# The first token group of an mLSTM and SwiGLU kernel: k and q of both halves loaded first, the weight loads all asked for by SP, and the first group's steps in another order

## The chip, the cores and the metric

The kernel runs on one core of one Trainium2 chip. The metric is the device time in microseconds (us) of one execution. The kernel before takes 515.06 us, the median of three runs (513.95, 515.06, 515.78).

## What is computed

An mLSTM cell over 4 batches, 8 heads, 768 tokens and 40 features, and a SwiGLU block on its output:

```python
for t in range(S):
    m_new = np.maximum(f_gate[:, :, t] + m, i_gate[:, :, t])
    f_stab = np.exp(f_gate[:, :, t] + m - m_new)
    i_stab = np.exp(i_gate[:, :, t] - m_new)
    C = f_stab * C + i_stab * outer(vt, kt)
    n = f_stab * n + i_stab * kt
    y[:, :, t] = sigmoid(o_gate[:, :, t]) * (C @ qt) / max(|n . qt|, 1)
...
x = y as (3072 tokens, 320)
out = (silu(x @ w_gate) * (x @ w_val)) @ w_out      # 320 -> 1536 -> 320
```

q, k, v and the gates arrive as float32, the three weight matrices as float64, that is as pairs of 32-bit words.

## The kernel before, in words

**Groups.** The 768 tokens of a batch are cut into six groups of 128. All four batches of a group are worked on together, so that a group has 32 heads (batch times head) and 512 tokens for the SwiGLU block. The 32 heads stand in two halves of 16, called P = 0 and P = 1 (the "pairs" of the change: two batches each); batch u has 8 of them. Group 0 starts from an empty state and has its own functions (first_...); groups 2 to 5 run in a steady loop at the end, which the change doesn't touch.

**Order.** The order of the instructions on every engine is the order of the program text (manual_schedule): each engine and each DMA-asking engine (SP, and in places ACT) takes its own instructions in that order and waits at each for what it needs. A DMA that SP can't ask for yet holds up all those that SP asks for later.

**Group 0.** f0 and i0 hold the gates of the first 128 tokens. From their sums and running maxima PE builds the exponents of the weight table in PSUM (first_mask, first_inputs, first_maxima), and ACT writes the exponentials into W0, which lies in the first eight rows of h_sb (first_exp). k and q of 16 heads are turned by PE (first_turn with 128x128 transposes; turn_one, used by group 1, with 64x64 ones) and copied to kT and qT. first_scores multiplies k and q on PE, and DVE multiplies the scores into W0. first_own multiplies W0 with the values v of batch u, first_x divides (DVE), first_gate multiplies by the sigmoid of o (sig, ACT), first_wrap's copy repeats 64 columns behind x, and a seam turns x on PE and copies it to xT. first_values and first_state make the state that group 1 starts from. burn(n) issues n products of zeros in bf16 that nobody reads.

**PSUM.** There are eight banks in two rings of four, tagged "cell" and "gen"; a bank is taken again when the work on its previous content is done.

**Weights.** The weights come in ten pieces, piece_load(p): pieces 0 and 1 hold one block (128 columns of w_gate and w_val, 640 KB in three DMAs), pieces 2 to 6 two blocks (1,280 KB in three DMAs), pieces 7 to 9 parts of w_out (1,280 KB in one DMA). w_gate goes into partitions 0 to 63, w_val into 64 to 127. A piece lands either in one of two rotating "raw" buffers or in a tile that is not in use yet (home). Block j is then rebuilt as float32 by convert(j): scale (ACT, two operations), join (DVE, two) and rounded (one integer addition on GpSimd or DVE).

**The blocks of group 0's SwiGLU.** hidden(0, m) multiplies xT with block m (L706, 20 records on PE), ACT takes the Silu (L711) and DVE the product (L712) into h_sb. Twelve such steps m = 0 to 11 run one after the other; in each, the conversions that ahead[m] names come before the Silu, and what slots[m] names comes behind: the preparation of group 1. Of that matter here: late_sums, late_maxima and late_decay (sums and maxima of the gates of tokens 128 to 767, from f_sb and i_sb), M_dram (the maxima written to DRAM by SP, L963), weights_load (SP reads M_dram back, spread over 64 partitions, into the two partition halves of w_sb, L484), turn (k and q of group 1, slots 5 and 6), weights_sub and weights_mask in slot 7 (DVE L488, GpSimd L493), weights_exp in slot 8 (ACT L512), the scores and weigh in slot 9 (PE L353, DVE L360), and do_add in slot 10 (PE L379). Then follow the remaining blocks, the projection (project_all, L723) and the loop over the later groups.

**Functions and lines that are spoken of:** load (L138), piece_load (L187), scale, join, rounded (L212 to L229), late_sums (L296 to L298), turn_one (L318), first_values (L552, L553), first_turn (L561), first_scores (L571, L575), first_own (L582), first_x (L587 to L590), first_gate (L596, L597), first_state (L604), first_seam (L616), sig (L515), burn (L521).

Of the kernel before, what the change touches and what calls it, by code (L numbers as in the profile page):

```python
# [18 lines left out]
L = 128  # L19
# [5 lines left out]
def kernel(  # L25
# [111 lines left out]
    def load(dst, a, c, P):  # L137
        nc.sync.dma_start(out=dst[:, heads(P), 0:D], in_=tokens(a, c, P))  # L138
# [7 lines left out]
    def gate_rows(a):  # L146
        return a.rearrange("b h s -> (b h) s")
# [3 lines left out]

    nc.scalar.dma_start(out=f0, in_=spread_rows(f_gate))
    nc.sync.dma_start(out=i0, in_=spread_rows(i_gate))
    nc.scalar.dma_start(out=flat(f_sb), in_=gate_rows(f_gate)[:, L:])
    nc.scalar.dma_start(out=flat(i_sb), in_=gate_rows(i_gate)[:, L:])


    raws = {}
    PIECES = [("gv", 0, 1), ("gv", 1, 1)] + [("gv", m, 2) for m in range(2, NFC, 2)] + [("o", m, 4) for m in range(0, NFC, 4)]

    def piece_load(p, home=None):
        kind, m, n = PIECES[p]
        if kind == "gv":
            a, d = NKC, n * 128
            gate_w, val_w = (w[:, m * 128:(m + n) * 128].rearrange("(c p) f -> p c f", p=HP) for w in (moe_w_gate, moe_w_val))
            src = [(slice(0, HP), slice(0, NKC), gate_w), (slice(HP, 128), slice(0, NKC - 1), val_w[:, 1:]),
                   (slice(HP, 128), slice(NKC - 1, NKC), val_w[:, 0:1])]
            queues = (nc.sync,) + 2 * (nc.scalar if p < 5 else nc.sync,)
        else:
            a, d = n, DM  # L170
            src = [(slice(0, 128), slice(0, n), moe_w_out[m * 128:(m + n) * 128].rearrange("(a p) d -> p a d", p=128))]
            queues = (nc.sync,)
        if src[0][2].dtype == F32:
            for r, cs, w in src:
                if kind == "o":
                    nc.sync.dma_start(out=wo_sb[r, m:m + n, :], in_=w)
                else:
                    for x in range(n):
                        nc.sync.dma_start(out=wgv_sb[r, m + x, cs], in_=w[:, :, ts(x, 128)])
            return  # L180
        if home is None:
            raw = conv.tile([128, 4 * NKC * 128], U32, name="raw")
        else:
            raw = home.rearrange("p a t -> p (a t)").bitcast(U32)
        raw = raw[:, 0:2 * a * d]
        for (r, cs, w), queue in zip(src, queues):
            queue.dma_start(out=raw[r].rearrange("p (a d) -> p a d", a=a)[:, cs], in_=w.bitcast(U32))  # L187
# [43 lines left out]
    def convert(j, eng=None):  # L231
        scale(j)
        join(j)
        rounded(j, eng)

    for P in range(2):
        load(k_sb, k, 0, P)
        load(q_sb, q, 0, P)
        load(v_sb, v, 0, P)
    load(o_sb, o_gate, 0, 0)  # L240


    junk = early.tile([128, 512], BF16)
# [51 lines left out]
    def late_sums():  # L295
        nc.vector.tensor_tensor_scan(flat(f_sb), flat(keep1), flat(f_sb), 0.0, op0=ALU.mult, op1=ALU.add)  # L296
        nc.gpsimd.memset(step1, 0.0)
        nc.gpsimd.tensor_sub(i_sb, i_sb, f_sb)  # L298

    def late_maxima():  # L300
        nc.vector.tensor_copy(step1[:, 0:1, 0:1], f0[0:BH, end].unsqueeze(1))
# [8 lines left out]
    M_dram = tc.dram_tile([BH, S - L], F32, name="M_dram")  # L310


    def turn_one(P, src, dst, engs):
        tp = [bank("tp_kq").rearrange("p (a t) -> p a t", t=SUB) for _ in range(2)]
        for a in range(UA):
            h = P * UH + 2 * a
            for i in range(2):
                nc.tensor.transpose(tp[i][:, a, :], src[half(i), h:h + 2, :].rearrange("p h d -> p (h d)"),  # L318
                                    ident[half(i), half(i)])
        for i in range(2):  # L320
            copy(engs[i], dst[:, P * UA:(P + 1) * UA, half(i)], tp[i])
# [143 lines left out]
    def xT(n):  # L465
        return xT_sb

    def seam(n, P, engs):
        engs = list(engs)
        dst = xT(n).rearrange("p c (u i s) -> p c u i s", u=B, i=2)  # L470
        for cs in (range(0, 4), range(4, NKC)):
# [76 lines left out]

    w_end = early.tile([128, BH, 1], F32)

    def first_values(P):
        nc.gpsimd.tensor_copy(w_end[:, heads(P)], W0[:, heads(P), end])  # L552
# [26 lines left out]
    def first_own(u):  # L579
        first_y[u] = bank("first_y", "gen")[:, 0:H * D1].rearrange("p (h d) -> p h d", d=D1)  # L580
        for h in range(H):
            nc.tensor.matmul(first_y[u][:, h, :], lhsT=W0[:, u * H + h, :], rhs=v_sb[:, u * H + h, :], start=True, stop=True)  # L582

    def first_x(u):
        y = first_y.pop(u)
# [21 lines left out]
    def first_kept(P, ps, eng):  # L607
        copy(eng, state(2)[:, P * UA:(P + 1) * UA], ps)

    def first_seam(P, engs):  # L610
        for c, eng in zip(range(0, NKC, 2), engs):
            cs = range(c, min(c + 2, NKC))
            tp = bank("tp_x")[:, 0:len(cs) * 2 * L].rearrange("p (c u s) -> p c u s", u=2, s=L)
            for w in cs:
                for b in range(2):
                    nc.tensor.transpose(tp[:, w - c, b, :], x_sb[:, 2 * P + b, ds(w * HP, 2 * HP)], ident)  # L616
            copy(eng, xT(0)[:, c:c + len(cs), 2 * P * L:(2 * P + 2) * L].rearrange("p c (u s) -> p c u s", u=2), tp)
# [12 lines left out]
    first_own(0)  # L630
    late_sums()
    first_turn(1, k_sb, kT, (A, A))
    first_x(0)
    first_turn(1, q_sb, qT, (A, V))
    load(o_sb, o_gate, 0, 1)
    piece_load(0)
    first_own(1)
    first_values(1)
    first_scores(1)
    first_x(1)  # L640
    sig(0)
    piece_load(1)
    burn(3)
    first_own(2)
    piece_load(2, h_sb[:, 1:1 + NKC])
    sig(1)
    burn(2)
    first_own(3)
    first_gate(0)
    first_x(2)  # L650
    first_x(3)
    first_gate(1)
    first_seam(0, (A, A, V))
    scale(0)
    ps1 = first_state(1, "gen")
    burn(1, "gen")
    piece_load(3, h_sb[:, NH - NKC:])
    join(0)
    first_seam(1, (A, A, V))
    rounded(0, V)  # L660
    first_kept(0, first_state(0), A)
    first_kept(1, ps1, V)
    convert(1, V)
    nc.scalar.activation(warm, warm, AF.Silu)
    piece_load(4, wo_sb)
    piece_load(5)


    pair = early.tile([BH, PP], F32)
# [289 lines left out]
    def load_all(dst, a, n):  # L959
        for P in range(2):  # L960
# [147 lines left out]
```

## Time and profile before

| what | value |
|---|---|
| median of three runs | 515.06 us (513.95 to 515.78) |
| the profiled execution's own time | 513.3 us |
| its span, first to last instruction | 511.5 us |
| PE (matmul) busy | 505.1 us, 99% |
| PE weight loads busy | 428.8 us, 84% |
| DVE / ACT / GpSimd busy | 332.3 / 204.8 / 255.0 us |
| DMA moved | 43.27 MB in 205,497 packets, 193,432 of them under 512 B |
| first product of group 0's SwiGLU (L706) | 31.92 us |

The profile is one execution on the chip; times are from the span's start. PE is TensorE's matmuls, PEld its weight loads, DVE VectorE, ACT ScalarE, POOL GpSimd, SP the engine that asks for DMAs; a trailing q is an engine's sequencer. A row of a timeline has start, busy time, engine, line, operation, what is written and read, the count, and in brackets the idle time ahead of it with what ended it. A row of the windows view has the stretch, its length, the busy time of each engine with the number of instructions, PE's granted clock, the DMA engines' mean busy share (packets overlap, so it can be over 1) and GB/s. q, k, v and o come in rows of 160 bytes, the weights in rows of 1,024 or 2,048, so a transfer of the same size can take different times. "To landing" in the view of DMA issues is the time from an issue to the last part of its data.

### The profile page before, as it was taken

The page shows a single profiled execution, that of the slowest core. Times are in us where ns is not written, and L with a number is a line of the kernel's source. Part 1 is how long each engine was busy: PE and PEld are TensorE (multiplying, and loading weights), DVE is VectorE, ACT ScalarE, POOL GpSimd, SP SyncE. Part 2 cuts the span into 40 slices and gives each one's busy share as a digit, 9 for nine tenths or more (in the row PEclk, how much of TensorE's full clock was granted, in tenths as well). Part 3 has the DMA queues.
Part 4 walks back from the last instruction along what each step waited for, and adds up shares of the span by engine and source line. Part 5 has one row for each costly group of instructions (what it writes and reads, how often), then busy time and mean ns, then how long its engine had stood idle before and what let it go on. Part 6 is the DMA issues. An engine that isn't in the chain of part 4 may idle for free.

```text
span 511.5 us, 14788 instructions
## 1 busy us (share of the span) xinstructions
PE 505.1 (99%) x6307; PEld 428.8 (84%) x6309; DVE 332.3 (65%) x539; ACT 204.8 (40%) x394; POOL 255.0 (50%) x274
## 2 busy tenths in 40 slices
PE   8999999999999999999999999999999999999997
PEld 4964445667888899988899888899988899988896
DVE  5779767887897777687466678467658554233421
ACT  3477655448512339312339321338421340223210
POOL 1303427475879663367652457652447650166710
PEclk9999999999999999999999999999999999999999
DMA  9999999698502992501993411993101200000001
GB/s 123 174 232 238 168 194 244 148 177 119 88 1 45 143 130 39 92 3 26 156 134 42 75 21 27 156 131 43 42 3 19 37 3 27 27 1 0 1 14 38
DMA packets 205497, 43.27 MB, mean 85 GB/s; under 512 B 193432, under 2 KB 200600, under 8 KB 205432
## 3 DMA queue, kind: packets, MB, share of 16 engines
q1 hardware_dynamic: 203444, 39.49, 49.4%
q10 hardware_dynamic: 1988, 2.85, 2.4%
q8 instruction: 49, 0.80, 0.7%
q14 instruction: 16, 0.13, 0.1%
HBM read 35.68 MB, written 4.01 MB: 78 GB/s over the span
## 4 chain that ended last, share of the span: by engine, by line
PE 91%; DMA 2%; DVE 2%; issue 1%; POOL 1%; ACT 1%; SPq 0%; DVEq 0%; ACTq 0%; POOLq 0%
PE gv_x L854 26%; PE o_ps L777 23%; PE gv_y L854 21%; PE gv_ps L706 5%; PE o_ps L723 5%; DMA w_sb<-M_dram 2%; PE inter L402 2%; PE intra L411 2%; PE sp L353 2%; PE first_y L582 1%; PE add L379 1%; POOL w_sb L493 1%; PE burn L521 1%; PE tp_kq L561 1%; PE sp L571 1%
## 5 line engine op out<-in xcount | busy, mean ns | idle before, releaser
L854 PE MATMUL gv_x<-xT,wgv_sb 64*128 64x256 f32 x720 | 89.1, 377 | 0.0
L854 PEld LDWEIGHTS gv_x<-xT,wgv_sb 64*128 64x128 f32 x720 | 69.6, 187 | 7.9 <-issue 0.2
L777 PE MATMUL o_ps<-wo_sb,h_sb 128*128 128x160 f32 x480 | 67.4, 300 | 0.0
L777 PEld LDWEIGHTS o_ps<-wo_sb,h_sb 128*128 128x128 f32 x480 | 65.6, 190 | 1.7 <-issue 1.7
L902 ACT ACTIVATE h_sb<-gv_x 128x256 f32<-128x256 f32 x30 | 11.5, 383 | 117.8 <-PE gv_x L854 117.8
L706 PE MATMUL gv_ps<-xT,wgv_sb 64*128 64x512 f32 x240 | 53.7, 596 | 0.3 <-DVE wgv_sb L229 0.3
L706 PEld LDWEIGHTS gv_ps<-xT,wgv_sb 64*128 64x128 f32 x240 | 23.6, 187 | 24.4 <-issue 23.2
L854 PE MATMUL gv_y<-q_sb,wgv_sb 64*128 64x256 f32 x360 | 44.0, 377 | 0.0
L854 PE MATMUL gv_y<-xT,wgv_sb 64*128 64x256 f32 x360 | 43.9, 376 | 0.0
L854 PEld LDWEIGHTS gv_y<-q_sb,wgv_sb 64*128 64x128 f32 x360 | 34.9, 187 | 4.2 <-DVE tmp L894 0.4
L854 PEld LDWEIGHTS gv_y<-xT,wgv_sb 64*128 64x128 f32 x360 | 35.0, 187 | 3.9
L364 POOL TENSOR_TENSOR vw_sb<-v_sb,w_sb 128x656 f32<-128x656 f32 x10 | 14.6, 1467 | 41.2 <-ACT w_sb L509 40.0
L777 PE MATMUL o_ps<-wT,S 128*128 128x160 f32 x240 | 33.4, 299 | 0.0
L777 PEld LDWEIGHTS o_ps<-wT,S 128*128 128x128 f32 x240 | 32.9, 190 | 0.0
L509 ACT ACTIVATE w_sb<-w_sb,g_T 128x64 f32<-128x64 f32 x128 | 31.0, 334 | 0.0
L854 PE MATMUL gv_x<-q_sb,sw 64*128 64x256 f32 x240 | 31.0, 376 | 0.0
L875 POOL TENSOR_TENSOR h_sb<-x_sb 128x512 f32<-128x512 f32 x12 | 15.8, 1314 | 24.6 <-ACT x_sb L874 24.6
L895 POOL TENSOR_TENSOR tmp<-tmp 128x512 f32<-128x512 f32 x15 | 20.0, 1332 | 14.5 <-DVE tmp L894 14.5
L875 POOL TENSOR_TENSOR h_sb<-tmp 128x512 f32<-128x512 f32 x13 | 16.5, 1269 | 21.5 <-ACT tmp L874 21.5
L744 POOL TENSOR_TENSOR S<-h_sb 128x256 f32<-128x256 f32 x30 | 22.6, 752 | 9.2 <-DVE h_sb L875 7.3
L854 PE MATMUL gv_y<-q_sb,sw 64*128 64x256 f32 x200 | 27.0, 388 | 0.0
L723 PE MATMUL o_ps<-wo_sb,h_sb 128*128 128x320 f32 x96 | 26.9, 437 | 0.0
(221 smaller groups left out, 984.6 us busy)
## 6 DMA issues: line engine op xcount, KB each, us to landing
w_sb<-M_dram SPq DMA_DIRECT2D x10, 512.0 KB, 7.1
k_sb<-in_k_dram SPq DMA_DIRECT2D x12, 320.0 KB, 7.4
v_sb<-in_v_dram SPq DMA_DIRECT2D x12, 320.0 KB, 5.5
o_sb<-in_o_gate_dram SPq DMA_DIRECT2D x12, 320.0 KB, 6.8
raw<-in_moe_w_out_dram SPq DMA_DIRECT2D x3, 1280.0 KB, 7.5
x_sq<-k_sb SPq DMA_DIRECT2D x64, 40.0 KB, 2.0
q_sb<-in_q_dram SPq DMA_DIRECT2D x32, 64.0 KB, 3.8
out_dram<-tmp SPq DMA_DIRECT2D x24, 80.0 KB, 1.7
```

Source lines behind the costliest of these rows:

```text
L353: nc.tensor.matmul(sp[two][half(i), a, :], lhsT=kT[feats(two), P * UA + a, half(i)], rhs=qT[feats(two), P * UA + a, half(i)], start=True, ...
L364: eng.tensor_tensor(vw_sb[:, heads(P)], v_sb[:, heads(P)], w_sb[:, heads(P), last].to_broadcast([128, UH, D1]), op=ALU.mult)
L402: nc.tensor.matmul(inter[two][half(i), a, :], lhsT=qT[feats(two), P * UA + a, half(i)], rhs=state(2 * n + i)[feats(two), P * UA + a, :], s ...
L509: nc.scalar.activation(w_sb[:, h], w_sb[:, h], AF.Exp, bias=g_T[:, n, h:h + 1], scale=-1.0)
L706: nc.tensor.matmul(ps[i], lhsT=wgv_sb[half(i), m, kc, :], rhs=x[half(i), kc, :], start=(kc == 0), stop=(kc == NKC - 1))
L723: nc.tensor.matmul(ps[u], lhsT=hid(g, m)[:, ts(u, L)], rhs=wo_sb[:, m, :], start=(m == 0), stop=(m == NFC - 1))
L744: eng.tensor_tensor(S1[:, k], lo[:, second_half], hi[:, second_half], op=ALU.add)
L777: nc.tensor.matmul(node[x][:, i], lhsT=lhs(k)[:, ts(i, L)], rhs=rhs(k), start=start and k == 0 and i == 0, stop=stop and k == KH - 1, skip ...
L854: nc.tensor.matmul(ps[:, i, cols], lhsT=lhs(c)[half(i)], rhs=rhs(c)[half(i)], start=start and c == 0, stop=stop and c == n - 1, skip_group ...
L875: (nc.vector if k == KH - 1 else nc.gpsimd).tensor_tensor(h_sb[:, 2 * k + 1], uw[:, 0], uw[:, 1], op=ALU.mult)
L895: nc.gpsimd.tensor_tensor(uw[:, :, second_half], uw[:, :, second_half], uw[:, :, first_half], op=ALU.add)
L902: nc.scalar.activation(h[:, first_half], x[:, 0, first_half], AF.Silu)
```

## The change

Loads: the gates of the later tokens (f_sb, i_sb) go from the front of ACT's queue to a place behind piece 1 on SP; k and q of both halves are asked for first, then v of both, then o's first half, piece 0, o's second half, piece 1, the later gates, and pieces 2, 3 and 4. All of these are asked for ahead of any work, and all parts of every piece by SP (before, ACT asked for w_val of pieces 0 to 4, each piece at a place between the steps of group 0). Piece 1 shares piece 0's raw buffer; piece 2's home is the back part of wo_sb. Piece 5 moves to slot 0.

Steps: the scores of both halves come ahead of the products with the values; the second half is turned by turn_one; first_own does each head in two column halves; half of the gates go to GpSimd; the seam is made of 64x64 transposes; late_sums, late_maxima, M_dram, late_decay, late_turns and decay move to later slots.

```diff
-    nc.scalar.dma_start(out=flat(f_sb), in_=gate_rows(f_gate)[:, L:])
-    nc.scalar.dma_start(out=flat(i_sb), in_=gate_rows(i_gate)[:, L:])
...
-            queues = (nc.sync,) + 2 * (nc.scalar if p < 5 else nc.sync,)
+            queues = (nc.sync,) + 2 * (nc.sync,)
...
-            raw = conv.tile([128, 4 * NKC * 128], U32, name="raw")
+            if p == 1:
+                raw = ring[0][:, 2 * NKC * 128:]
+            else:
+                raw = ring[p] = conv.tile([128, 4 * NKC * 128], U32, name="raw")
...
+    for dst, a in ((k_sb, k), (q_sb, q)):
+        load(dst, a, 0, 0)
+    for dst, a in ((k_sb, k), (q_sb, q)):
+        load(dst, a, 0, 1)
     for P in range(2):
-        load(k_sb, k, 0, P)
-        load(q_sb, q, 0, P)
         load(v_sb, v, 0, P)
     load(o_sb, o_gate, 0, 0)
+    spare_wo = wo_sb.rearrange("p m d -> p (m d)")[:, H * L:H * L + 4 * NKC * 128].rearrange("p (a t) -> p a t", a=1)
+    for p, home in ((0, None), (1, None), (2, spare_wo), (3, h_sb[:, NH - NKC:]), (4, None)):
+        piece_load(p, home)
+        if p == 0:
+            load(o_sb, o_gate, 0, 1)
+        if p == 1:
+            nc.sync.dma_start(out=flat(f_sb), in_=gate_rows(f_gate)[:, L:])
+            nc.sync.dma_start(out=flat(i_sb), in_=gate_rows(i_gate)[:, L:])
...
-        nc.gpsimd.tensor_sub(i_sb, i_sb, f_sb)
+        nc.vector.tensor_sub(i_sb, i_sb, f_sb)
...
-            nc.tensor.matmul(first_y[u][:, h, :], lhsT=W0[:, u * H + h, :], rhs=v_sb[:, u * H + h, :], start=True, stop=True)
+            for i in range(2):
+                nc.tensor.matmul(first_y[u][half(i), h, :], lhsT=W0[:, u * H + h, half(i)], rhs=v_sb[:, u * H + h, :],
+                                 start=True, stop=True)
...
-    def first_gate(P):
-        for u in (2 * P, 2 * P + 1):
-            x = x_sb[:, u, 0:DM].rearrange("p (h d) -> p h d", d=D)
-            nc.vector.tensor_tensor(x, x, o_sb[:, u * H:(u + 1) * H], op=ALU.mult)
+    def first_gate(u, eng):
+        x = x_sb[:, u, 0:DM].rearrange("p (h d) -> p h d", d=D)
+        eng.tensor_tensor(x, x, o_sb[:, u * H:(u + 1) * H], op=ALU.mult)
...
-    burn(7)
+    burn(5)
...
     first_exp(0)
+    first_end(0)
     first_turn(0, k_sb, kT, (V, V))
     first_turn(0, q_sb, qT, (A, V))
     first_exp(1)
+    first_end(1)
+    first_scores(0)
+    turn_one(1, k_sb, kT, (A, A))
+    turn_one(1, q_sb, qT, (V, A))
     first_values(0)
-    first_scores(0)
+    burn(2, "gen")
+    first_scores(1)
     first_own(0)
-    late_sums()
...
+    first_own(1)
+    first_x(0)
+    first_x(1)
+    first_values(1)
+    sig(0)
+    scale(0)
+    sig(1)
+    first_gate(0, G)
+    first_gate(1, G)
+    first_wrap(0)
+    first_own(2)
+    first_own(3)
+    burn(1)
+    first_x(2)
+    join(0)
+    first_x(3)
+    rounded(0, G)
+    seam(0, 0, (A, A, A, A))
+    first_gate(2, V)
+    first_gate(3, V)
+    first_wrap(1)
+    states = [first_state(P, "gen") for P in range(2)]
+    burn(2)
+    seam(0, 1, (A, V, A, V, A, A), (0, 2, 4, NKC))
+    first_kept(0, states[0], A)
+    first_kept(1, states[1], V)
...
-        0: [run(convert, 2, V), run(late_maxima), run(load_all, k_sb, k, 1),
-            run(nc.sync.dma_start, out=M_dram, in_=flat(M_sb)), run(load_all, q_sb, q, 1)],
-        1: [run(piece_load, 6), run(late_decay)],
-        2: [run(nc.scalar.activation, step1, step1, AF.Exp), run(decay_rows), run(weights_load, 1), run(load_all, v_sb, v, 1)],
-        3: [run(late_turns)],
-        4: [run(decay), run(cap_table)],
+        0: [run(convert, 2, V), run(piece_load, 5), run(load_all, k_sb, k, 1), run(load_all, q_sb, q, 1)],
+        1: [run(late_sums), run(piece_load, 6, spare_wo)],
+        2: [run(late_maxima), run(nc.sync.dma_start, out=M_dram, in_=flat(M_sb))],
+        3: [run(late_decay), run(nc.scalar.activation, step1, step1, AF.Exp), run(decay_rows), run(weights_load, 1), run(load_all, v_sb, v, 1)],
+        4: [run(late_turns), run(cap_table)],
         5: [run(turn, 0, (A, A), (A, V))],
         6: [run(turn, 1, (A, A), (A, V)), run(piece_load, 7)],
-        7: [run(weights_sub, 1, 0), run(weights_mask, 0), run(weights_sub, 1, 1), run(weights_mask, 1), run(nc.gpsimd.memset, q_sb, 0.0)],
+        7: [run(decay), run(weights_sub, 1, 0), run(weights_mask, 0), run(weights_sub, 1, 1), run(weights_mask, 1), run(nc.gpsimd.memset, q_sb, 0.0)],
```

More of the change, by code (lines that the diff above doesn't have):

```diff
@@ L153 @@
     nc.sync.dma_start(out=i0, in_=spread_rows(i_gate))
-    nc.scalar.dma_start(out=flat(f_sb), in_=gate_rows(f_gate)[:, L:])
-    nc.scalar.dma_start(out=flat(i_sb), in_=gate_rows(i_gate)[:, L:])
     raws = {}
+    ring = {}
     PIECES = [("gv", 0, 1), ("gv", 1, 1)] + [("gv", m, 2) for m in range(2, NFC, 2)] + [("o", m, 4) for m in range(0, NFC, 4)]
@@ L310, with turn_one @@
     M_dram = tc.dram_tile([BH, S - L], F32, name="M_dram")
-    def turn_one(P, src, dst, engs):
-        tp = [bank("tp_kq").rearrange("p (a t) -> p a t", t=SUB) for _ in range(2)]
+    def turn_one(P, src, dst, engs, tag="cell"):
+        tp = [bank("tp_kq", tag).rearrange("p (a t) -> p a t", t=SUB) for _ in range(2)]
         for a in range(UA):
@@ L466, in xT, with seam @@
         return xT_sb
-    def seam(n, P, engs):
+    def seam(n, P, engs, parts=(0, 4, NKC)):
         engs = list(engs)
         dst = xT(n).rearrange("p c (u i s) -> p c u i s", u=B, i=2)
-        for cs in (range(0, 4), range(4, NKC)):
+        for cs in (range(a, b) for a, b in zip(parts, parts[1:])):
             tp = [bank("tp_x")[:, 0:len(cs) * L].rearrange("p (c u s) -> p c u s", u=2, s=SUB) for _ in range(2)]
@@ L549, with first_end @@
     w_end = early.tile([128, BH, 1], F32)
+    def first_end(P):
+        nc.gpsimd.tensor_copy(w_end[:, heads(P)], W0[:, heads(P), end])
     def first_values(P):
-        nc.gpsimd.tensor_copy(w_end[:, heads(P)], W0[:, heads(P), end])
         nc.gpsimd.tensor_tensor(vw_sb[:, heads(P)], v_sb[:, heads(P)], w_end[:, heads(P)].to_broadcast([128, UH, D1]),
@@ L591, in first_x, with first_wrap @@
                                 den.to_broadcast([128, H, D]), op=ALU.mult)
-    def first_gate(P):
-        for u in (2 * P, 2 * P + 1):
-            x = x_sb[:, u, 0:DM].rearrange("p (h d) -> p h d", d=D)
-            nc.vector.tensor_tensor(x, x, o_sb[:, u * H:(u + 1) * H], op=ALU.mult)
+    def first_gate(u, eng):
+        x = x_sb[:, u, 0:DM].rearrange("p (h d) -> p h d", d=D)
+        eng.tensor_tensor(x, x, o_sb[:, u * H:(u + 1) * H], op=ALU.mult)
+    def first_wrap(P):
         nc.gpsimd.tensor_copy(x_sb[:, 2 * P:2 * P + 2, DM:], x_sb[:, 2 * P:2 * P + 2, 0:HP])
@@ L608, in first_kept @@
         copy(eng, state(2)[:, P * UA:(P + 1) * UA], ps)
[L610 to L617, printed above, removed]
-    burn(7)
+    burn(5)
     banks = [(u, j) for j in range(2) for u in range(B)]
@@ L627 @@
     first_exp(1)
+    first_end(1)
+    first_scores(0)
+    turn_one(1, k_sb, kT, (A, A))
+    turn_one(1, q_sb, qT, (V, A))
     first_values(0)
-    first_scores(0)
+    burn(2, "gen")
+    first_scores(1)
     first_own(0)
-    late_sums()
-    first_turn(1, k_sb, kT, (A, A))
+    first_own(1)
     first_x(0)
[L634 to L637, printed above, removed]
+    first_x(1)
     first_values(1)
-    first_scores(1)
-    first_x(1)
     sig(0)
-    piece_load(1)
-    burn(3)
-    first_own(2)
-    piece_load(2, h_sb[:, 1:1 + NKC])
-    sig(1)
-    burn(2)
[L648 to L662, printed above, removed]
+    scale(0)
[3 more added lines that the diff above has]
+    first_wrap(0)
+    first_own(2)
+    first_own(3)
[9 more added lines that the diff above has]
+    states = [first_state(P, "gen") for P in range(2)]
+    burn(2)
+    seam(0, 1, (A, V, A, V, A, A), (0, 2, 4, NKC))
+    first_kept(0, states[0], A)
+    first_kept(1, states[1], V)
     convert(1, V)
     nc.scalar.activation(warm, warm, AF.Silu)
-    piece_load(4, wo_sb)
-    piece_load(5)
     pair = early.tile([BH, PP], F32)
```

## The prediction

> **What bounds the kernel now.** I read the page's head, then the timelines of PE, SP and the other engines for the first 110 us, then the DMA views. The page's slices:
>
> ```profile
> span 511.5 us, 14788 instructions
> PE   8999999999999999999999999999999999999997
> DMA  9999999698502992501993411993101200000001
> ```
>
> PE is busy in every slice, and the DMA engines are busy through the first seven (90 us). PE's timeline from the first gate/value product (L706) on:
>
> ```profile
> 31.92 17.46 PE L706 MATMUL gv_ps<-xT,wgv_sb 64*128 64x512 f32 x80 [0.28 <-DVE wgv_sb L229]
> ...
> 59.40 0.66 PE L318 MATMUL tp_kq<-ident,k_sb 64*128 64x64 f32 x16
> ...
> 80.78 4.56 PE L706 MATMUL gv_ps<-xT,wgv_sb 64*128 64x512 f32 x20
> 85.27 0.31 PE L379 MATMUL add<-vw_sb,k_sb 64*64 64x41 f32 x2
> 85.78 2.33 PE L379 MATMUL add<-vw_sb,k_sb 64*64 64x41 f32 x126 [0.20 <-DVE w_sb L360]
> ```
>
> From 31.92 to 85.27 PE has no gap: one block m of hidden() costs it 4.36 us (17.46 / 4). At 85.78 it waits, for DVE's weigh(). The chain behind that wait, from the timeline of all engines:
>
> ```profile
> 72.75 2.36 DVE L488 TENSOR_TENSOR w_sb<-g_T,w_sb 128x1024 f32<-128x1024 f32 x2 [0.89 <-DMA w_sb<-M_dram]
> ...
> 74.05 6.76 POOL L493 TENSOR_SCALAR_AFFINE_SELECT w_sb<-w_sb 64x1024 f32<-64x1024 f32 x4 [11.97 <-DVE w_sb L488]
> ...
> 80.84 1.06 ACT L512 ACTIVATE w_sb<-w_sb 128x1024 f32<-128x1024 f32 x1 [2.29 <-POOL w_sb L493]
> ...
> 81.91 1.28 ACT L711 ACT_TABLE_LOAD   x1
> 83.21 0.60 ACT L711 ACTIVATE tmp<-gv_ps 128x512 f32<-128x512 f32 x1
> ...
> 84.44 2.47 DVE L360 TENSOR_TENSOR w_sb<-sp,w_sb 128x512 f32<-128x512 f32 x4
> ```
>
> The second half of w_sb lands at 72.66 (issued 59.96, 12.7 to landing, the longest of its line's view); subtraction, mask, exponential, table load, Silu and weigh() follow without a pause, and add() starts 13.1 us after the landing. So two chains end together there: PE's own work, with about 0.5 us to spare, and **the landing of w_sb plus 13.1**. Behind 86 us PE is full again, so a shift of add() is a shift of the end.
>
> **The start, part by part.** Each DMA's landing is its issue plus the time in the issue view. In before, o_sb's first half, the seventh of the 160-byte loads, lands at 21.2 (14.34 + 6.9), and such loads follow each other by 2.15 us (159 GB/s in 12 to 19). The later gates (160 KB, some 0.5 us at the 368 GB/s that rows of 2,560 bytes reach in 75 to 82) no longer lie ahead: the seven are down at 20.7 in the order k, q, k, q, v, v, o.
> - PE up to scores(0): two burns fewer (2 x 0.43), but k's transposes wait for ACT's exponentials to free banks; 0.6 earlier. PE isn't the limit later, for o_sb's second half is.
> - first_own in column halves: 32 records for 16. The nearest row, L604 (columns of 64), does 32 in 1.13 us, L582 16 in 1.88: 0.75 saved in each of four, or up to 1.9 lost if a half costs a whole. Hidden under the loads both ways; without that cover the four would give 3.0 or take 7.6.
> - turn_one for pair 1 (L318: four times 0.49 us for 64 records) for first_turn (32 in 2.1): nothing. Two gates and a rounding on POOL (0.9 estimated for 128x320, between L744's 0.75 for 256 and L875's 1.31 for 512; 1.55 for L229): beside the wait below. late_sums (1.47 DVE, 0.62 and 1.53 POOL) leaves the start and comes back in slot 1 as 1.47 and some 0.8 of DVE (L308's form), under PE's products.
> - o_sb's second half now lies behind piece 0: 20.7 + 3.2 + 2.15 = 26.1. Then sig(1) 0.74, two gates on DVE 0.98 behind first_x(3), transposes and the first pair of seam copies 0.8: **first product at about 29.4, 2.5 us earlier** (1.0 to 3.5).
>
> **The weights.** What does a piece cost on SP's queue alone? The windows view and the queues' shares (DMA view of the same windows):
>
> ```profile
> 36.00:42.00 6.00, 6.00 (x32) 3.10 (x30) 4.68 (x8) 4.06 (x6) 0.00 (x0) 1.00 1.05 326
> 43.00:48.00 5.00, 5.00 (x26) 2.20 (x24) 4.90 (x11) 4.38 (x6) 2.44 (x2) 1.00 1.07 210
> 60.00:65.00 5.00, 5.00 (x48) 2.58 (x46) 3.73 (x6) 3.09 (x7) 1.55 (x1) 1.00 1.05 207
> ```
>
> The last column is GB/s. In 36 to 42 SP's queue has 57.8% and ACT's 47.4%: 326 GB/s. In the other two SP's works alone on the same kind of rows, with further loads in flight behind: 210 and 207. The change gives all pieces to SP. So 640 KB take 3.2 us and 1,280 KB 6.4 (piece 6: 61.6 to 68.0). Landings after: piece 0 at 23.9, o 26.1, piece 1 29.3, later gates 29.9, piece 2 at 36.3, piece 3 at 42.7, **piece 4 at 49.1; before it was 45.3** (29.55 + 15.7). By the windows 3.8 us are lost. The Trainium skill says otherwise (DMA: Bandwidth & Descriptors, Issuing engines are not separate DMA queues): issuing from several engines saves only the sequencer's time, since all run on the same 16 DMA engines. By that rule the stream loses nothing; that is a rival below.
>
> The gain at the start then goes in three places. Block 2 needs piece 2: before, landing 36.3, ready 40.1 (scale, join, rounding 3.8). After, the same 40.1, so the third block starts at 40.2 instead of 40.65: **0.4 is left of 2.5**. Piece 5 then takes 6.8 (as 45.3 to 52.1) and the next k and q 9.3 (52.1 to 61.6 less M_dram): turn(0) in slot 5 needs q's first half at 55.9 + 6.2 = 62.1, while PE comes there at about 58.5: **a new wait of 3.6**. Piece 6 lands at 55.9 + 9.3 + 6.4 = 71.6.
>
> **M_dram's place.** SP's timeline of before:
>
> ```profile
> 51.29 2.12 SPq L963 DMA_DIRECT2D M_dram<-M_sb  x1
> 53.45 2.37 SPq L138 DMA_DIRECT2D q_sb<-in_q_dram  x2
> 55.92 1.99 SPq L187 DMA_DIRECT2D raw<-in_moe_w_gate_dram  x1
> 57.96 1.28 SPq L187 DMA_DIRECT2D raw<-in_moe_w_val_dram  x2
> 59.33 8.22 SPq L484 DMA_DIRECT2D w_sb<-M_dram  x2
> ```
>
> M_dram was asked for ahead of q and piece 6 and had landed when w_sb was asked for; w_sb then flowed right behind piece 6, 4.6 us after it (68.0 to 72.66). After, M_dram comes in slot 2, behind piece 6 of slot 1, and is the instruction just ahead of w_sb. It lies behind piece 6 in the same queue, lands about 0.3 behind it, and only then may SP ask for w_sb; v, the out-weights and o are queued behind on SP. From an empty queue the two halves take 7.6 us (asked for at 100.06, second landing at 107.6): 3.0 us more than 4.6, with M_dram itself 3.4. w_sb lands at 71.6 + 0.3 + 0.1 + 7.6 = **79.6, 7.0 later than 72.66**. decay's move to slot 7 and late_turns' to slot 4 (PE 0.8 in all, DVE 1) lie ahead of that wait.
>
> DVE stands at the subtraction in slot 7 until then, with block 8's product queued behind, so block 10's products wait for their banks (ready 7.8 after the landing, 87.4; PE is through at about 84): a second wait of some 3.4. add() starts at 79.6 + 13.1 = 92.7 instead of 85.78. The early start changes nothing in that.
>
> **Sum.** The profiled execution took 513.3 us for a span of 511.5: 513.3 + 7.0 = 520.3. Its time is 1.8 under the median of the runs, 515.06, which gives **522.1**. The queue's rate for 38 us of pieces (5% of it is 1.9) and the price of w_sb (5.1, the first half's, to 7.6) give 519 to 525.
>
> **Rivals.**
> - *One queue is as quick as two.* Then piece 6 lands at 68.0 less 0.3, and only M_dram's place costs: w_sb at 67.7 + 8.0 = 75.7, 3.0 late: 518.1 (517 to 519). For it: 28 to 36 had both queues and moved only 216. Against: 326 against 210.
> - *Faster: SP's queue, with all loads behind each other, reaches 326 by itself.* Then pieces 0 to 4 take 16.1 us instead of 25.6, piece 6 lands near 57, w_sb at 65, and the start's 2.5 us are kept: 512.5. It decides from the point where w_sb lands at 72.66 again, that is with 7.0 us less for 7,680 KB, about 250 GB/s. For it: out-weights in 75 to 82 reach 368 from one queue, though into all 128 partitions; against it: 210 and 207 in two stretches, with several loads in flight.
> - *The waits turn PE's clock down.* At the start of this trace weight loads of the burns lie 0.43 us apart until 5.43 us and closer after, as if the array ran at half speed until then. A 3.4 us wait before block 10 could bring that back: half speed through 3.4 us loses 1.7, of which weigh()'s chain hides 0.9: 523 to 526. The Trainium skill (TensorE: Matmul & The Clock Gate, The HAM clock gate) has such a gate, with a window of about 3.4 us; no row here shows it after the start.
>
> **Chances.** Forecast 0.62, one queue as two 0.18, faster 0.10, clock 0.10. A difference under 0.3% (1.5 us) can't be told from none in this kernel. Of the faster rival's 0.10, 0.09 lies beyond that bound; its rest and the low edge of the first rival (0.03) make 0.04 for the same; 0.87 stays for slower. The range, leaving out the faster rival and the extremes of the clock: 516.5 to 525.8.
>
> **What would show it.** Right: SP's queue near 210 GB/s from 24 to 50; piece 4 near 49; PE idle before L318 near 58 and before L706 near 84, the latter behind DVE L488 waiting for w_sb; w_sb asked for only when M_dram is down. Wrong: GB/s near 300 in 30 to 45, w_sb down before 73, or add() (L379) before 86.

## The result, and the profile after

The changed kernel takes 520.66 us (median of six runs, 520.09 to 524.45); the kernel before, run beside it, 514.50 us (six runs, 511.99 to 515.78). The ratio is 1.0137, with a 95% interval of 1.0096 to 1.0178: about 6 us slower. The profiled execution took 521.38 us for a span of 519.6, 8.1 us over before's 511.5. The head of the page after:

```profile
span 519.6 us, 14989 instructions
...
PE   8888799999899999999999999999999999999997
...
DMA  9999989899610995230995220895100200100001
```

PE falls to 7 in the fifth slice (52 to 65 us) and to 8 in the eleventh (130 to 143), where before had a 9. The DMA row stays at 8 or 9 through ten slices. PE's timeline (start, busy us, line, what is written and read, count, idle before):

```profile
30.41 8.84 PE L712 MATMUL gv_ps<-xT,wgv_sb 64*128 64x512 f32 x40
40.90 13.15 PE L712 MATMUL gv_ps<-xT,wgv_sb 64*128 64x512 f32 x60 [1.64 <-DVE wgv_sb L231]
...
63.39 0.71 PE L330 MATMUL tp_kq<-ident,q_sb 64*128 64x64 f32 x16 [2.63 <-DMA q_sb<-in_q_dram]
...
86.62 4.56 PE L712 MATMUL gv_ps<-xT,wgv_sb 64*128 64x512 f32 x18 [0.50 <-DVE h_sb L718]
91.34 0.31 PE L391 MATMUL add<-vw_sb,k_sb 64*64 64x41 f32 x2 [0.17 <-DVE w_sb L372]
...
141.46 1.14 PE L860 MATMUL gv_x<-xT,wgv_sb 64*128 64x256 f32 x8 [2.09 <-DVE C L407]
```

The first product comes 1.51 us earlier than before (30.41 for 31.92); the third block starts 0.25 later than before's 40.65, because block 2 waits for its rounded weights. q holds turn(0) for 2.63 us. add() starts at 91.34, 6.07 after before's 85.27 (its main part, 91.94, 6.16 after). The row at 141.46 shows a second wait, of 2.09 us. In before PE runs through the same place:

```profile
133.31 1.46 PE L854 MATMUL gv_x<-xT,wgv_sb 64*128 64x256 f32 x12
```

The windows of the changed kernel (GB/s last) and SP's timeline and waits:

```profile
36.00:40.00 4.00, 3.26 (x16) 1.38 (x12) 1.59 (x3) 1.51 (x3) 0.00 (x0) 1.00 1.06 208
```
```profile
64.05 0.53 SPq L969 DMA_DIRECT2D M_dram<-M_sb  x1
71.56 2.08 SPq L496 DMA_DIRECT2D w_sb<-M_dram  x2
```
```profile
SPq L496 <- DMA M_dram<-M_sb: 6.9, 1, 6.9
```

SP's queue alone moves 208 GB/s here (208 to 220 in every stretch of 4 us from 28 to 52), where two queues moved 326 before. M_dram is asked for at 64.05 behind piece 6, and SP stands 6.9 us until it is down before it may ask for w_sb. Now the second wait: DVE's rows around the update of C in before, and then in after:

```profile
127.98 2.37 DVE L343 STREAM_TRANSPOSE kT<-raw 128x1024 f32<-128x1024 f32 x2 [3.54 <-DMA out_dram<-x_sb]
130.27 1.99 DVE L395 TENSOR_TENSOR C<-C,add 40x328 f32<-40x328 f32 x4
```
```profile
136.00 2.37 DVE L355 STREAM_TRANSPOSE kT<-raw 128x1024 f32<-128x1024 f32 x2 [5.56 <-DMA raw<-in_k_dram]
138.29 3.02 DVE L407 TENSOR_TENSOR C<-C,add 40x328 f32<-40x328 f32 x6
```

These transposes need k of group 2, which early_squares loads (L337 before, L349 after) in 16 requests on SP. DVE does them 8.02 us later: the first request is issued 5.06 later (121.95 for 116.89), the 16 take 1.58 longer, and the last takes 3.48 to land instead of 2.10. (Before's row names out_dram as what ended its wait; its last square landed at 127.76, 0.2 us ahead of the transposes.) C is updated behind them, and PE waits for that. The chain of waits of after, in order of time:

```profile
119.13 2.42 POOL wo_sb L231
...
132.30 3.48 DMA raw<-in_k_dram
```

SP's request ahead of the squares (group 2's o_sb) waits for a rounding of out-weights on GpSimd, and the chain then runs over the squares' issue and the last landing into the rows above. Up to the first request this is PE's own delay handed on: PE's second add() (L391) is 5.46 us behind before's (131.21 for 125.75), and the squares are asked for 5.06 later. What makes PE wait is that the requests take longer and the last lands slowly. So the profiled execution pays at two places: 6.1 us at add() and 2 more here.

### The profile page after: what moved, and what is told of

Its sections match the earlier page's. It is cut to its first block, busy times and chain, and to the rows that moved or that the text cites. A ratio compares the mean times of both kernels' runs of the same rounds, so it can differ in the third digit from the quotient of the medians.

```text
span 519.6 us, 14989 instructions
## 1 busy us (share of the span) xinstructions
PE 502.4 (97%) x6406; PEld 423.6 (82%) x6406; DVE 333.7 (64%) x537; ACT 204.9 (39%) x398; POOL 256.8 (49%) x276
## 4 chain that ended last, share of the span: by engine, by line
PE 76%; DMA 3%; SPq 3%; DVE 2%; POOL 1%; issue 1%; ACT 1%; DVEq 0%; ACTq 0%
PE gv_x L860 24%; PE o_ps L783 22%; PE gv_y L860 20%; PE o_ps L729 3%; PE inter L414 2%; SPq L349 2%; PE intra L423 2%; PE sp L365 2%; DMA M_dram<-M_sb 1%; DMA v_sb<-in_v_dram 1%; PE add L391 1%; PE gv_ps L712 1%; POOL w_sb L505 1%; DVE C L407 1%; DMA raw<-in_k_dram 1%
## 5 line engine op out<-in xcount | busy, mean ns | idle before, releaser
L712 PE MATMUL gv_ps<-xT,wgv_sb 64*128 64x512 f32 x240 | 55.0, 596 | 2.1 <-DVE wgv_sb L231 1.6
```

Of the source, the lines that this page charges most:

```text
L712: nc.tensor.matmul(ps[i], lhsT=wgv_sb[half(i), m, kc, :], rhs=x[half(i), kc, :], start=(kc == 0), stop=(kc == NKC - 1))
```

## The experiments

The theory: all loads run through SP, M_dram's landing among them, and every one behind is late; the kernel pays where PE needs them. The main rivals: a part of the computation itself (the start, first_own in halves) costs the time, or the clock does.

**M_dram alone, in the kernel before (e4).** M_dram is asked for behind piece 6, as in the change.

```diff
-            run(nc.sync.dma_start, out=M_dram, in_=flat(M_sb)), run(load_all, q_sb, q, 1)],
-        1: [run(piece_load, 6), run(late_decay)],
+            run(load_all, q_sb, q, 1)],
+        1: [run(piece_load, 6), run(nc.sync.dma_start, out=M_dram, in_=flat(M_sb)), run(late_decay)],
```

> The kernel before with M_dram alone moved behind piece 6 (from slot 0 to slot 1). Theory: piece 6 lands at 68 as before, M_dram right behind it, SP waits for it and w_sb takes 7.6 us from there: 75.7 to 76 instead of 72.66, add() 3.0 to 3.4 later, time 517.5 to 518. Rival (add() has room, or the queue fills the gap): 514.5, within 0.3%.

Measured: 516.82 us against 514.38, ratio 1.0053 (1.0020 to 1.0087). w_sb was asked for at 67.52 and landed at 75.07, 2.41 later than in before; add() started at 87.60. M_dram's place costs 2.4 us: a cause, and a smaller one than expected. The profiled execution, 519.86 us, was one of the longest; it has the second wait too:

```profile
87.60 0.31 PE L379 MATMUL add<-vw_sb,k_sb 64*64 64x41 f32 x2 [0.17 <-DVE w_sb L360]
...
139.10 2.08 PE L854 MATMUL gv_x<-xT,wgv_sb 64*128 64x256 f32 x8 [2.67 <-DVE C L395]
```

**All parts asked for by SP, in the kernel before (e5).**

```diff
-            queues = (nc.sync,) + 2 * (nc.scalar if p < 5 else nc.sync,)
+            queues = 3 * (nc.sync,)
```

> The kernel before with one change: SP asks for all three parts of pieces 0 to 4, at the same places of the program. Theory (one queue moves these rows at about 210 GB/s, two together at up to 326): no stretch of 36 to 44 us goes over 225 GB/s, piece 4 lands near 49 instead of 45.3, block 2 near the same 36 to 37, and q, piece 6 and w_sb each come 3 to 4 us later: w_sb near 76, time 517.5 to 518.5. Rival (the number of queues makes no difference, as the Trainium skill's page DMA: Bandwidth & Descriptors, section Issuing engines are not separate DMA queues, has it): piece 4 stays at 45 to 46 and the time at 514.4.

Measured: 519.04 us against 514.21, ratio 1.0095 (1.0066 to 1.0123). Windows and PE of this kernel:

```profile
36.00:42.00 6.00, 6.00 (x31) 3.10 (x29) 4.15 (x7) 4.07 (x6) 0.00 (x0) 1.00 1.06 212
```
```profile
62.49 0.71 PE L318 MATMUL tp_kq<-ident,q_sb 64*128 64x64 f32 x16 [1.89 <-DMA q_sb<-in_q_dram]
...
88.46 0.31 PE L379 MATMUL add<-vw_sb,k_sb 64*64 64x41 f32 x2 [0.18 <-DVE w_sb L360]
```

The stretch that ran at 326 GB/s with two queues runs at 212 with one, with no other edit. The wait for q appears, w_sb lands at 75.93 (3.27 later) and add() comes 3.2 later; C is updated at 137.06 (6.8 later). This one word costs 4.8 us, the larger part of the change's price. (With M_dram's 2.4 it comes to 7.3, more than the 6.2 of the whole change: the two don't simply add.) The rule of the Trainium skill (DMA: Bandwidth & Descriptors, Issuing engines are not separate DMA queues) would have left the time as it was.

**first_own's halves alone, in the kernel before (e8).**

```diff
-            nc.tensor.matmul(first_y[u][:, h, :], lhsT=W0[:, u * H + h, :], rhs=v_sb[:, u * H + h, :], start=True, stop=True)
+            for i in range(2):
+                nc.tensor.matmul(first_y[u][half(i), h, :], lhsT=W0[:, u * H + h, half(i)], rhs=v_sb[:, u * H + h, :],
+                                 start=True, stop=True)
```

> The kernel before with first_own's column halves alone, which the changed kernel's trace shows at 0.98 us for a batch instead of 1.88. Theory (the landing of piece 2, block 2's conversion and w_sb end the first 86 us, not PE's start): the first L706 may come up to 2 us earlier, but block 2 is ready near 40 and add() starts near 85.7 as before; the time stays within 0.3% of before. Rival (PE bounds the start, as its 91% of the chain says): the 3.6 us of PE work are gone from the end too, 510.6 to 511.5.

Measured: 516.16 us against 515.26, ratio 1.0007 (0.9979 to 1.0035); first product at 31.9, add() at 86.28. The halves neither cost nor bring anything: the loads cover them.

**Undoing the parts in the changed kernel (e1, e2, e3).** e1 moves piece 6 behind M_dram; e2 lets ACT ask for w_val of pieces 2 to 4 at three places of the start; e3 does both.

```diff
-        1: [run(late_sums), run(piece_load, 6, spare_wo)],
-        2: [run(late_maxima), run(nc.sync.dma_start, out=M_dram, in_=flat(M_sb))],
+        1: [run(late_sums)],
+        2: [run(late_maxima), run(nc.sync.dma_start, out=M_dram, in_=flat(M_sb)), run(piece_load, 6, spare_wo)],
```
```diff
-            queues = (nc.sync,) + 2 * (nc.sync,)
+            queues = (nc.sync,) + 2 * (nc.scalar if 2 <= p < 5 else nc.sync,)
...
-    for p, home in ((0, None), (1, None), (2, spare_wo), (3, h_sb[:, NH - NKC:]), (4, None)):
+    for p, home in ((0, None), (1, None)):
...
+    piece_load(2, spare_wo)
...
+    piece_load(3, h_sb[:, NH - NKC:])
...
+    piece_load(4)
```

> The changed kernel with piece 6 moved from slot 1 to the end of slot 2, so that M_dram is asked for ahead of it as before. Theory (the loss is M_dram's place plus the single queue's rate): w_sb is asked for without a wait and its second half lands about 4.6 us behind piece 6, near 76.2 instead of 78.8; add() starts near 89.2 and the time falls by about 2.7, to 518.0. Rival (one queue is as quick as two, the place is all of the loss): w_sb lands near 72.7 and the time is that of before, 514.5. Rival (the new order of the start is the loss): nothing changes, 520.7.

> The changed kernel, but ACT asks for w_val of pieces 2, 3 and 4, at three places between the steps of the start; M_dram stays behind piece 6. Theory: with both queues the weights flow at about 320 GB/s for some us, piece 4 lands near 46 instead of 49.8, all that follows on SP's queue comes 3 to 4 us earlier, w_sb lands near 75.3, and the time falls by 3.5 to about 517. Rival (the number of queues makes no difference): piece 4 stays near 49.5 and the time at 520.7.

> The changed kernel with both: M_dram ahead of piece 6, and ACT asking for w_val of pieces 2 to 4. Theory: w_sb lands near 72.5, add() starts near 85.6, and only the new start is left of the change: 513.5 to 514.5, within 0.3% of before. If the new start has a cost of its own, it stays above 516; if its gain of 1.5 us outlives block 2's wait, 513 or less.

Measured, against 514.38: e1 519.94 (1.0109, 1.0046 to 1.0173), e2 520.06 (1.0108, 1.0065 to 1.0152), e3 520.65 (1.0119, 1.0077 to 1.0162). None won back what was expected. In e1 w_sb was asked for at 64.92 but landed at 77.48, only 1.3 earlier, and the wait for q, now over three microseconds, was followed by slow products. Windows and PE of e1:

```profile
64.00:68.00 4.00, 4.00 (x12) 1.82 (x11) 2.82 (x4) 1.89 (x3) 0.65 (x1) 0.57 0.97 210
```
```profile
63.23 0.71 PE L330 MATMUL tp_kq<-ident,q_sb 64*128 64x64 f32 x16 [3.38 <-DMA q_sb<-in_q_dram]
63.75 6.24 PE L712 MATMUL gv_ps<-xT,wgv_sb 64*128 64x512 f32 x20
```

A block that takes 4.54 us took 6.24, at a granted clock of 0.57, so PE came to add() at 91.0 by its own work. In e2 the rate rose as the theory has it (296 and 311 GB/s in 36 to 40 and 40 to 44), and piece 5 landed at 52.84 instead of 56.74; but SP had asked for w_gate of three pieces ahead, ACT's w_val of piece 2 landed at 42.2 only, block 2 waited until 46.16, and the clock was down twice (0.50 in 32 to 36, behind a wait of 2.40 us at the start; 0.84 in 44 to 48, behind the 2.65 us before block 2). In e3 w_sb was down at 72.89, where before had it, and add() still started at 92.3, because PE had lost that time at the start and at block 2 (first product 32.80, third block 45.84). These three show that the landing of w_sb is one chain of two, PE's own work being the other; they do not test the start by itself, for the edit of e2 and e3 made the start and piece 2 late.

**GpSimd as the second queue (e10, e11).** e10 is e1 with w_val of pieces 0 to 6 asked for by GpSimd, those of 0 to 4 at places of the start; e11 is before with that of pieces 5 and 6. The edit of e10 and that of e11:

```diff
+            ask(src[0], nc.sync)
+            if len(src) > 1:
+                pend[p] = lambda: [ask(x, nc.gpsimd) for x in src[1:]]
```
```diff
-            queues = (nc.sync,) + 2 * (nc.scalar if p < 5 else nc.sync,)
+            queues = (nc.sync,) + 2 * (nc.scalar if p < 5 else nc.gpsimd,)
```

> The changed kernel with M_dram ahead of piece 6, and GpSimd asking for w_val of pieces 0 to 6 at places of the start and the slots where it has little to do, SP for w_gate as now, so that both halves of the partitions are written at once from about 15 us on. Theory (the rate is set by whether both halves are written, the loss by the late stream): stretches near 300 GB/s between 20 and 45 us, piece 2 down by 33 and piece 4 by 42, no wait before block 2, q in time, w_sb before 72.7; add() starts at 84 to 85.5 and the time is 511 to 514.5, at or below before. Rival (a queue that GpSimd writes itself is slow, or its other work is held up): val lands later than gate, block 2 waits longer than in the changed kernel, 520 or more.

> The kernel before with GpSimd asking for w_val of pieces 5 and 6 in place of SP. Theory: those two pieces take 4 us each instead of 6.4, w_sb lands 3 to 5 us earlier than 72.66, but PE itself is through its blocks only at 85.3, so add() gains at most 0.5: 514 to 515, within 0.3%. Rival (w_sb's landing had more weight than the 0.5 us shows, or the later squares of k come earlier too): faster by 1.5 us or more.

Both missed: 523.97 (1.0179, 1.0151 to 1.0207) and 521.89 (1.0145, 1.0089 to 1.0201), against 514.72. In e10 w_val went ahead of v and o, and the first product came at 41.1. In e11 piece 5's went ahead of the pieces before it. PE's timeline of e11:

```profile
46.63 11.12 PE L706 MATMUL gv_ps<-xT,wgv_sb 64*128 64x512 f32 x40 [5.22 <-DVE wgv_sb L229]
```

ACT's own request for piece 4 had to wait 7.3 us for an earlier landing, by its waits, with block 2's scale() queued behind it, and PE stood 5.22 us. A second queue pays only if it keeps the order in which the pieces are needed.

**Another order on SP (e7, e9).** In the changed kernel SP asks, behind piece 4, for k, q, M_dram, piece 5, w_sb, piece 6, v; all parts stay on SP. The blocks of these pieces are converted a step later. e9 also puts the later gates behind piece 2.

```diff
-    ahead.update({4: [6], 5: [7, 8], 6: [9], 7: [10], 8: [11], 9: [], 10: [], 11: []})
+    ahead.update({4: [6], 5: [7], 6: [8], 7: [9], 8: [10], 9: [], 10: [], 11: []})
...
+        2: [run(late_maxima), run(nc.sync.dma_start, out=M_dram, in_=flat(M_sb)), run(piece_load, 5)],
+        3: [run(late_decay), run(nc.scalar.activation, step1, step1, AF.Exp), run(decay_rows), run(weights_load, 1), run(piece_load, 6, spare_wo), run(load_all, v_sb, v, 1)],
...
+        9: [run(do_scores), run(do_weigh, 0), run(do_weigh, 1), run(do_decayed, 2), run(load_all, o_sb, o_gate, 1), run(convert, 11, V)],
```
```diff
-        if p == 1:
+        if p == 2:
```

> The changed kernel, all loads still by SP alone, but in another order behind piece 4: k, q, M_dram, piece 5, w_sb, piece 6, v; blocks 8, 9 and 10 are converted one step later and block 11 behind weigh(). Theory (the loss is late data, and which data is late depends on the order of the one queue): q's first half lands near 56, no wait before the second half of turn(0); w_sb lands near 70.5 instead of 78.8, piece 6 near 77; add() starts between 86 and 88 instead of 91.9 and the time is 515 to 517, though one queue still moves the weights at 210 GB/s. Rival (the steps of the new start are the loss): 519 or more.

> As the kernel with the reordered queue, and the later gates (160 KB) behind piece 2 instead of piece 1. Theory: piece 2 lands 0.8 us earlier (near 36.8), the wait before block 2 (1.6 us idle in the changed kernel) shrinks by as much, and the time is 0.8 below that of the reordered queue. Rival (nothing hangs on block 2, as a later wait ends the stretch): no difference between the two.

Measured, against 515.26: e7 519.74 (1.0090, 1.0060 to 1.0120), e9 520.53 (1.0101, 1.0073 to 1.0129). PE of e7:

```profile
86.23 2.08 PE L391 MATMUL add<-vw_sb,k_sb 64*64 64x41 f32 x128
...
138.59 2.08 PE L860 MATMUL gv_x<-xT,wgv_sb 64*128 64x256 f32 x8 [2.99 <-DVE C L407]
```

For the first 86 us the theory holds: no wait for q, w_sb down at 70.25, add() at 86.23, 0.96 over before, though one queue carries everything. Yet the span is still 5.8 over before's, and the time is above the 515 to 517 expected. PE is 1.7 late at its second add() (127.44 for 125.75), of which 1.06 is a wait for the last block's weights, converted later in this order. Then the second wait has grown to 2.99, with C updated at 135.42 (before 130.27). Behind it the clock was down, and the products up to 143.28 took 1.5 us longer than in before; the window (clock third from the end):

```profile
138.00:142.00 4.00, 3.41 (x18) 3.10 (x20) 3.67 (x6) 0.42 (x1) 3.84 (x6) 0.57 0.71 80
```

In e9 the wait before block 2 fell from 1.87 to 0.89 and nothing was won at the end: a later wait decides. That left the question whether the squares of k hold this by themselves.

**The squares ahead of o (e12).** e7 with one exchange:

```diff
-        3: [run(do_divide, 1, 1), run(load_all, o_sb, o_gate, 2), run(early_squares, 0), run(weights_cap, 0)],
+        3: [run(do_divide, 1, 1), run(early_squares, 0), run(load_all, o_sb, o_gate, 2), run(weights_cap, 0)],
```

> The kernel of e7 (SP's order behind piece 4: k, q, M_dram, piece 5, w_sb, piece 6, v) with one more exchange: the squares of k for group 2 (L349) are asked for ahead of group 2's o_sb load (L138) and not behind it. In e7 SP asks for the o_sb load until 120.02 and for the squares from 120.02 to 131.3; the last lands at 132.9, the update of C (L407) follows at 135.42 and PE waits 2.99 us at 138.59. Theory (the rest of the change's cost comes in at the squares of k, which SP asks for late): the squares are asked for from about 114.7, the last lands between 126 and 129, C is updated at 129 to 131, PE's wait at 138.59 is gone, and the span falls by about 3 us from 517.3 to 514 to 515 (a time near 516.7, 0.3% over the kernel before, where e7 was 0.9% over it). add() stays at 86.2. Rival (the squares are late but something behind them, such as the weight table or the o_sb load itself, is as late): PE waits about as long a little further on and the span stays within 0.7 us of 517.3.

Measured: 515.36 us (12 runs) against 513.95, ratio 1.0017 (0.9986 to 1.0048); span 513.2, 4.1 under e7's. DVE and PE of e12:

```profile
128.53 2.37 DVE L355 STREAM_TRANSPOSE kT<-raw 128x1024 f32<-128x1024 f32 x2 [1.94 <-DMA raw<-in_k_dram]
130.82 4.06 DVE L407 TENSOR_TENSOR C<-C,add 40x328 f32<-40x328 f32 x8
```
```profile
135.48 1.46 PE L860 MATMUL gv_x<-xT,wgv_sb 64*128 64x256 f32 x12
```

The first request went out at 115.22 instead of 120.02, the last landed at 128.11, C was updated 4.6 us earlier, and PE, whose row has no idle time ahead of it, runs through. With SP's order mended at these two places the changed kernel cannot be told from before, with one queue for all pieces and all the new steps of the start in it. So the loss lies in the order and the landing of loads; a cost of the computation that the change rearranged, if there is one, lies within the interval (up to 0.5%). The same exchange was not tried in the kernel before, so a gain that before would share is not excluded; its profile has little to spare there (the estimate of half a us below). No kernel of the study beats before.

**The rate by itself (e6).** Loads of weight rows alone, all rows of 2,048 bytes, 2,560 KB in each of five patterns. Of these the first, second and fifth:

```diff
+    gate_to(SP, one_queue[:, x], 2 * x, every)
+    val_to(SP, one_queue[:, x], 2 * x, every)
...
+    gate_to(SP, two_queues[:, x], 2 * x, every)
+    val_to(ACT, two_queues[:, x], 2 * x, every)
...
+    SP.dma_start(out=all_rows[:, m], in_=src)
```

> No part of the computation: the kernel only loads weight rows of 2,048 bytes, 2,560 KB in each of five ways one after the other, and writes zeros. (1) SP alone, w_gate into partitions 0 to 63, then w_val into 64 to 127; (2) SP w_gate beside ACT w_val; (3) SP and ACT together into the same half, first both w_gate, then both w_val; (4) SP alone, a fifth of w_gate and a fifth of w_val by turns; (5) SP alone, rows of the same length into all 128 partitions. If two queues make the rate: (1), (4) and (5) at about 205 GB/s, (2) and (3) at 300 or more. If it is the two halves of the partitions being written at once: (1) and (3) at about 205, (2) and (5) at 300 or more, (4) between. If neither: all at one rate.

The windows view of e6 (GB/s last):

```profile
8.00:18.00 10.00, 4.77 (x3) 10.00 (x4) 1.00 1.07 225
26.00:28.00 2.00, 0.00 (x0) 0.00 (x0) 1.00 0.84 208
32.00:36.00 4.00, 0.96 (x1) 0.00 (x0) 1.00 0.97 322
...
44.00:50.00 6.00, 0.00 (x0) 0.00 (x0) 1.00 1.07 226
56.00:66.00 10.00, 0.96 (x1) 0.00 (x0) 1.00 0.68 204
72.00:78.00 6.00, 0.00 (x0) 0.00 (x0) 1.00 1.04 390
```

One queue writing the lower and then the upper 64 partitions: 225. Two queues, SP below and ACT above: 208 while only SP's packets moved, 322 once both halves were written at once. (Both queues were asked at 24.21, but SP's first transfer landed at 30.15 and ACT's at 33.26: two queues write both halves at once only where their transfers overlap. Before's 28 to 36 us, with both queues, moved 216.) Two queues into the same half: 226, no better than one. One queue by turns between the halves: 204, but here the DMA engines were busy for 0.68 only and SP's own asking, 128 KB every 0.64 us, was the limit, so this pattern settles nothing. One queue into all 128 partitions: 390. What makes the rate is how many partitions are written at the same time; the second queue helped before because it wrote the other half.

## Why the prediction was right, and where it was not

- *The forecast* was 522.1; 520.66 came, by the mechanism that it named: late loads, and not slower steps.
- *One queue, 3.2 us for 640 KB*: right. Piece 4 landed at 49.79 (49.1 forecast, 45.29 in before), piece 6 at 71.38 (71.6). The rival by which one queue is as quick as two fell with e5, the faster rival with the 208 to 220 GB/s of after.
- *w_sb at 79.6*: it landed at 78.82, 6.16 late instead of 7.0. Taken apart, the queue costs 3.27 at this place (e5; 3.6 forecast) and M_dram's 2.41 (e4; 3.4 forecast). The mis-sized terms are small: in e4 the halves took 7.55 from asking to landing, as taken, but piece 6 was down at 67.05, 0.95 before the 68.0 of before, once M_dram no longer lay ahead of it (0.2 to 0.3 was taken); in after they took 7.26 (71.56 to 78.82).
- *add() 13.1 after the landing*: 91.94 is 13.12 after 78.82.
- *The start 2.5 earlier, 0.4 of it left at block 2*: it was 1.51 and nothing. o_sb's second half landed at 27.37, not 26.1. It made no difference, as forecast.
- *first_own saves 0.75*: four of them took 3.93 us, 0.98 for each instead of 1.88, a gain of 0.9 in each; e8 shows that it does not reach the end.
- *A wait of 3.6 for q*: 2.63, at the place named. *A second wait of 3.4 before block 10*: only 0.50. Block 10's banks were free 0.8 earlier (86.62 for 87.4). PE had lost about 1 us more than forecast on the way (1.64 at block 2, 0.82 at the gates' turn) and came to block 10 at 85.00 instead of 84, and two products of that block, 1.1 us, went ahead of the wait. The sum does not change, since the landing of w_sb sets it.
- *"Behind 86 us PE is full again, so a shift of add() is a shift of the end"*: **this step failed**. add() is 6.16 late and the span 8.1; in e7 add() is 0.96 late and the span 5.8. PE being full there did not mean that nothing else was close: the squares of k ended just in time in before. (In after the waiting product starts 3.17 us behind C's first update; before's would be free at 130.27 + 3.17 = 133.4, and PE, whose second add() is 5.4 us earlier there, would come at 139.4 - 5.4 = 134.0: an estimate of half a us to spare.) e12 shows that they are a second chain. In medians the change costs 6.2 us, not 8.1: before's profiled execution is 1.2 under its median and after's 0.7 over. Part of the squares' lateness was a slow last landing in the profiled execution, so what a usual execution of after pays there is not shown. Against the profiled execution (520.3 forecast, 521.38 measured) two errors went to opposite sides, w_sb taken 0.84 too late and the squares not counted, and that they nearly cancel is luck. Of the 1.4 us by which 522.1 missed the median, 0.84 is w_sb and 0.56 the median of before, 515.06 on record and 514.50 beside the change.
- *The clock as a rival*: no slow products in after, where the longest wait was 2.63 us. e2 (2.65), e4 (2.67), e7 (2.99), e1 (3.38) and e11 (5.22) have them behind their waits. So the mechanism exists in this kernel and does not need the 3.4 us that the rival assumed; that the profiled execution of after was spared was close, and in part luck.

## What to carry to other kernels

Before a queue is taken away, ask which partitions the two queues write: here one queue into one half of them moved 210 GB/s, and two queues writing both halves at once 320. Where a queue becomes later, follow every later consumer of it, and not only the first that sets the end: a busy PE behind that point hides how close the next transfer is. A transfer that writes what the next one reads back from memory should be asked for ahead of large loads, not behind them.

## What the runs showed of the hardware

- **Rate by destination.** 204 to 226 GB/s into 64 partitions, 322 into both halves at once by two queues, 390 into all 128 by one (e6), with the same DMA engines about as busy (0.84 to 1.07, the pattern by turns apart). The Trainium skill (DMA: Bandwidth & Descriptors, Rules for kernel authors) says of two transfers to disjoint halves of the partitions that they serialize; 322 against 225 speaks against it where the two overlap, while its advice to use one transfer into 128 partitions agrees with the 390.
- **The clock comes down after a wait in the middle of the kernel.** After idle stretches of 3.4 us (e1) and 5.2 us (e11) PE's granted clock was 0.57 (64 to 68) and 0.50 (46 to 50), and the block behind e1's took 6.24 us instead of 4.54. Shorter waits did it too: behind 2.67 us in e4 and 2.99 in e7 it was 0.61 and 0.57 in 138 to 142. After 2.63 us (the changed kernel) and 2.38 (e5) it was 1.00. In e1, e4 and e7 it stood at 0.50 for 3.4 us (64.46 to 67.87, 138.90 to 142.32, 138.19 to 141.61). The Trainium skill (TensorE: Matmul & The Clock Gate, The HAM clock gate) has the clock come down after an idle window of about 3.4 us: the length of these stretches agrees with such a window, but waits of 2.67 and 2.99 us were enough here.
- **A request can hold the engine that makes it.** In these traces the requests of SP and ACT use eight landing signals in turn, and one waits until the request eight before it has landed, whichever of the two asked (GpSimd's in e10 and e11 have signals of their own): ACT stood 7.3 us for that in e11.
- **Code loads share the DMA engines.** A 16 KB packet of the instruction queue lay among the last squares of k in after, e4 and e5 (133.60, 131.38 and 132.48 us); their last landings took 3.5, 4.4 and 4.3 us from the request, against 2.1 in before, where such a packet came just behind them (127.78). That the packet held them was not tried by itself.
